# Attention into a feed-forward layer in float32: k of the first batch on ScalarE's queue, units laid out by segment first, the last stores cut into 32 rows

## The chip, the cores and the metric

The kernel runs on one core of one Trainium2 chip. The metric is device time in microseconds, the median of several executions. One execution was also taken by the hardware profiler. Its page and its trace are what is read here. The engines are called as in the profile: PE (matrix engine), PEld (its weight loads), DVE, ACT, POOL, and SP, which only issues transfers. "SPq" and "ACTq" are the queues of these engines' sequencers.

## What is computed

The inputs are q, k and v of 8 batches, 8 heads, 576 tokens and 64 channels. Two attentions are added and go through a feed-forward layer:

```python
q_d = q.reshape(B, H, Sd, factor, D).mean(axis=3)      # factor 4, the same for k and v
out_d = sm_attn(q_d, k_d, v_d)                         # attention of the means of 4 tokens
out_up = np.repeat(out_d, factor, axis=2)
mask = np.abs(pos[:, None] - pos[None, :]) < factor    # a window of 7 keys
scores = np.where(mask, scale * np.matmul(q, k.transpose(0, 1, 3, 2)), -1000000000.0)
...
x = (out_up + out_local).transpose(0, 2, 1, 3).reshape(B * S, H * D)
h = x @ w_in                                           # 512 -> 2048
g = np.maximum(h, 0.0) + alpha * np.minimum(h, 0.0)
out = g @ w_out                                        # 2048 -> 512
```

w_in and w_out come as 64-bit floats and are turned into pairs of 32-bit halves (high and low) on the chip.

## The kernel before, in words

**Layer.** The 4608 tokens are taken in 18 chunks of 256 (T), and the 2048 hidden channels in 8 pairs of 128, so 144 steps. A step makes h for two hidden blocks (`hidden`, L752: 24 matmuls, since the operands are split in high and low parts: xh, xl, wih, wil). Then ACT (`slopes`, L760 and L761), DVE (`larger`, L764) and ACT and POOL (`split`, L769 and the helper at L69) make gh and gl. `product` (L796) adds 12 matmuls into the chunk's two banks o (m = 0 and m = 1, 128 tokens each). After the eighth step of a chunk, `finish` copies both banks to sg on ACT (L802) and stores them on SP (L805). `rows` turns a stretch of tokens into addresses of the output. From token 576 on, tokens stand in units of 192, six runs of 32, so a store of 128 tokens has an address of three dimensions: 4 runs, 32 rows, 512 channels.

**Local attention.** Batch 0 is done at the start by PE (`first_batch`, four pairs of heads hp). The other batches are done by DVE in 21 units (u = 3 to 23) of 192 tokens. A unit has 128 partitions: four pairs of heads times 32 segments of 18 tokens. `load_q` and `load_kv` (L533, L552) load it, one transfer for each head of a pair (h2). `local` multiplies (L591), sums (L595) and weighs; PE transposes the result (`flip`, tile xp), and `join` (L671) adds the down part and writes xf, from which ACT and POOL make xh and xl. The first and last tokens of a sequence are masked by `build_masks`, which finds the partitions of the first and last segment.

**Down part.** `down` loads q, k and v of two heads in six transfers (tile ld, L232). POOL adds the groups of four tokens (`fold`, L72), and PE, ACT and DVE do the attention of the means.

**Start.** `load_pair` loads q, k (tile fqk, L393, runs of 64 channels) and v (fv, L396) of a pair of heads, `load_windows` the windows of v (vw). `ORDER` gives the order among these loads and those of the raw weights (L145, L149). ACT starts the decoding of the weights (temp, L184), and DVE does most of the rest (L188 to L211).

**What sets the order.** Up to the call of `tc.manual_schedule` a list scheduler places the instructions on each engine by its own estimate of times. Behind it, `events` is a list of times written out by hand, and every engine's order follows it. All transfers are issued by SP, in one order.

Of the kernel before, what the change touches and what calls it, by code (L numbers as in the profile page):

```python
# [50 lines left out]
def tile_attention_moe(ctx: ExitStack, tc: tile.TileContext, q, k, v, w_in, w_out, alpha, out):  # L51
# [29 lines left out]
    masks = {}  # L81

    def build_masks():
        for side, base in (("l", 0), ("r", -31)):
            pat = one.tile([128, 2, 7, 2, 3], F32, tag="lex", name=f"pat_{side}")
            nc.gpsimd.memset(pat, 0.0)
            for half in range(2):
                for dl in range(7):
                    js = [j for j in range(3)
                          if (3 * half + j + dl < 3 if side == "l" else 3 * half + j + dl >= 9)]  # L90
                    if js:
                        nc.gpsimd.memset(pat[:, half, dl, :, js[0]:js[-1] + 1], NEG)
            flag = one.tile([128, 4], F32, tag="flag", name=f"flag_{side}")
            nc.gpsimd.memset(flag, 0.0)
            nc.gpsimd.affine_select(out=flag, in_=flag, pattern=[[-32, 4]], base=base,
                                    channel_multiplier=1, compare_op=ALU.not_equal, fill=1.0)
            fl = one.tile([128, 1], F32, tag="fl", name=f"fl_{side}")
            nc.vector.tensor_reduce(out=fl, in_=flag, axis=AX.X, op=ALU.max)
            m = const.tile([128, 2, 7, 6], F32, name=f"mask_{side}")
            nc.vector.tensor_scalar(m.rearrange("p a b c -> p (a b c)"),  # L100
                                    pat.rearrange("p a b c d -> p (a b c d)"),
                                    fl[:, 0:1], None, op0=ALU.mult)
            masks[side] = m
# [259 lines left out]
    def first_batch(st):  # L363
# [25 lines left out]
        def load_pair(hp):  # L389
            qk[hp] = one.tile([72, 2, 8, 2, 64], F32, tag=f"spare{(4, 5, 0, 1)[hp]}", name=f"fqk{hp}")  # L390
            for i, src in enumerate((q, k)):
                for e in range(2):
                    nc.sync.dma_start(qk[hp][:, i, :, e, :],  # L393
                                      bass.AP(src.tensor, (2 * hp + e) * HEAD, [[512, 72], [64, 8], [1, 64]]))
            vt[hp] = st.tile([72, 2, 8, 64], F32, tag="vt", name=f"fv{hp}", bufs=3)
            nc.sync.dma_start(vt[hp].rearrange("p h t d -> p h (t d)"),  # L396
                              bass.AP(v.tensor, 2 * hp * HEAD, [[512, 72], [HEAD, 2], [1, 512]]))
# [132 lines left out]
    def load_q(u):  # L530
        qt = tiles[u, "q"] = late.tile([128, 2, 6, 64], F32, tag="qt", name=f"q{u}")
        for h2 in range(2):
            nc.sync.dma_start(qt[:, h2].rearrange("p t d -> p (t d)"),  # L533
                              bass.AP(q.tensor, unit_base(u) + h2 * HEAD,
                                      [[2 * HEAD, 4], [SEG * D, 32], [1, 384]]))

    def load_kv(u, x):
        src = k if x == "k" else v
        t = tiles[u, x] = late.tile([128, 2, 12, 64], F32, tag=f"{x}t", name=f"{x}{u}")
        for h2 in range(2):  # L540
            off = unit_base(u) + h2 * HEAD - 3 * D
            flat = t[:, h2].rearrange("p t d -> p (t d)")
            if u == 3 * B - 1 and h2 == 1:
                nc.vector.memset(flat[96:128, 576:768], 0.0)
                nc.sync.dma_start(flat[0:96], bass.AP(src.tensor, off,
                                                      [[2 * HEAD, 3], [SEG * D, 32], [1, 768]]))
                nc.sync.dma_start(flat[96:127], bass.AP(src.tensor, off + 6 * HEAD,
                                                        [[SEG * D, 31], [1, 768]]))
                nc.sync.dma_start(flat[127:128, 0:576],
                                  bass.AP(src.tensor, off + 6 * HEAD + 31 * SEG * D, [[1, 1], [1, 576]]))  # L550
            else:
                nc.sync.dma_start(flat, bass.AP(src.tensor, off,  # L552
                                                [[2 * HEAD, 4], [SEG * D, 32], [1, 768]]))

    def window(t, half, d0, nd):
        tok = 3 * half + d0
# [9 lines left out]
    def local(u, t0, t1):  # L566
# [94 lines left out]
        def join(i):  # L661
            j0, nt = groups[i]
            odv = od[b].rearrange("p a (s g) -> p a s g", g=9)
            tp = st.pop(("tp", i))
            xf = late.tile([128, 512], F32, tag="xf", name=f"xf{u}_{i}")[:, :128 * nt]
            xf = st["xf", i] = xf.rearrange("p (a t s) -> p a t s", a=4, s=32)
            for par in range(2):
                pos = [(18 * par + 6 * jj + j) // 4 for j in range(j0, j0 + nt)]
                for g in sorted(set(pos)):
                    k0, nk = pos.index(g), pos.count(g)  # L670
                    nc.vector.tensor_tensor(  # L671
                        xf.rearrange("p a t (s e) -> p e t a s", e=2)[:, par, k0:k0 + nk],
                        tp.rearrange("p (t a s e) -> p e t a s", t=4, a=4, e=2)[:, par, k0:k0 + nk],
                        odv[:, :, :, g].unsqueeze(1).to_broadcast([128, nk, 4, 16]), op=ALU.add)

        def place(i, low):
# [109 lines left out]
    def product(st):  # L786
        c, fp = divmod(st, NP)
        if fp == 0:
            outs[c] = [ps_o.tile([128, DM], F32, tag="po", name=f"o{c}_{m}") for m in range(T // 128)]
        gh, gl = gs.pop(st)  # L790
        for j in range(2):
            f = 2 * fp + j
            n, o = divmod(f, 4)
            for i, (g, w) in enumerate(((gh, 0), (gh, 1), (gl, 0))):
                for m, po in enumerate(outs[c]):
                    nc.tensor.matmul(po, g[:, j, 128 * m:128 * m + 128], wo[w][n][:, o, :],  # L796
                                     start=(f == 0 and i == 0), stop=(f == NF - 1 and i == 2))

    def finish(c):
        for m, po in enumerate(outs.pop(c)):  # L800
            sg = two.tile([128, DM], F32, tag="stage", name=f"sg{c}_{m}", bufs=SB)
            nc.scalar.copy(sg, po)  # L802
            row = 0
            for cnt, ap in rows(T * c + 128 * m, 128):
                nc.sync.dma_start(ap, sg[row:row + cnt, :])  # L805
                row += cnt

    def place_rest():
        hi, lo = (t[:, :, 0:S - 2 * T] for t in operand(2))
# [9 lines left out]
    with tc.tile_pool(name="start", bufs=1) as start:  # L819
# [20 lines left out]
        def at(t, f, *args):  # L840
            events.append((t, len(events), f, args))
# [5 lines left out]
    for s in range(NS):  # L847
        at(s - 1.95, hidden, s)
        at(s - 1.45, slopes, s)
        at(s - 1.15, larger, s)  # L850
        at(s - 1.0, split, s)
        at(s + 0.6, product, s)
        if s % NP == NP - 1:
            at(s + 1.02, finish, s // NP)

    blocks = [(w, fp, c) for w in range(2) for fp in range(N_EARLY, NP) for c in range(2)]
    at(-1.98, load_raw, 0, N_EARLY)
# [71 lines left out]
```

## Time and profile before

| | |
|---|---|
| median of three runs | 1025.86 us (1025.6 to 1030.05) |
| the profiled execution | 1026.39 us |
| its span, first to last instruction | 1024.5 us |
| PE busy | 960.5 us (94%) |
| DVE busy | 831.8 us (81%) |
| ACT busy | 560.4 us (55%) |
| POOL busy | 487.7 us (48%) |
| hardware queue of the transfers | 97.12 MB, 30.1% of 16 engines' span |
| granted clock of PE, mean | 0.969 |

The span is shorter than the execution's own time by what lies before the first and behind the last instruction, 1.9 us. A busy share is a mean over stages with different limits: the first 100 us (loads, decoding, batch 0), the long middle, and the last steps, in which only the layer is left. In a row of the trace stand the start, the duration, the engine, the line, the operation with its tiles and shapes, how many instructions are merged, and in brackets the idle time before it with what ended it. "A <- B" among the waits means that A's instruction stood until B's was done. A row of a stretch gives its length, the busy time of PE, PEld, DVE, ACT and POOL with their instructions, the granted clock, the mean busy share of the 16 DMA engines, and GB/s.

### The profile page before, as it was taken

To read this page: it belongs to the slowest core of one execution; us is meant where nothing else is said; L and a number is where in the kernel's file an instruction comes from. 1 tells how busy PE (TensorE), PEld (TensorE's weight loads), DVE (VectorE), ACT (ScalarE), POOL (GpSimd) and SP (SyncE) were. 2 spreads that over 40 slices of the span, in tenths; PEclk is the share of its full clock that TensorE was granted. 3 is DMA by queue.
4 is the path that set the end of the run, shared out by engine and by line. 5 is a ranking of instruction groups with operands and counts; after the bars stand their busy time and mean duration, and the time that the engine had idled before them with its cause. 6 is when DMAs were issued, how large, how long until landed. Compare 5 with 4: busy or idle time off the path is not lost.

```text
span 1024.5 us, 17852 instructions
## 1 busy us (share of the span) xinstructions
PE 960.5 (94%) x6402; PEld 853.0 (83%) x6402; DVE 831.8 (81%) x1346; ACT 560.4 (55%) x1484; POOL 487.7 (48%) x612
## 2 busy tenths in 40 slices
PE   4877989999999999999999999999999999999995
PEld 4756868898888899988888888888888898989894
DVE  6899978898788899899879888898898899995110
ACT  4767766465555554555555554655555564444442
POOL 2160645676565645555555544655555542333221
PEclk9956989999999999999999999999999999999998
DMA  8947343232322322322322232322322221100000
GB/s 184 228 141 246 111 126 110 96 109 85 115 100 95 106 75 86 109 93 102 107 84 74 92 107 77 116 90 80 104 98 81 93 78 62 73 36 21 1 21 20
DMA packets 59549, 98.25 MB, mean 96 GB/s; under 512 B 19910, under 2 KB 25286, under 8 KB 59462
## 3 DMA queue, kind: packets, MB, share of 16 engines
q1 hardware_dynamic: 59462, 97.12, 30.1%
q8 instruction: 50, 0.82, 0.3%
q14 instruction: 37, 0.30, 0.1%
HBM read 87.67 MB, written 9.44 MB: 95 GB/s over the span
## 4 chain that ended last, share of the span: by engine, by line
PE 74%; DVE 12%; DMA 4%; ACT 3%; issue 2%; SPq 2%; POOL 2%; ACTq 0%; DVEq 0%; POOLq 0%
PE h L752 34%; PE o L796 33%; PE s L263 2%; PE pv L297 2%; DVE temp L193 2%; DMA raw<-in_moe_w_in 1%; PE xp L659 1%; DMA ld<-in_v 1%; PE pT L287 1%; DVE temp L194 1%; DMA k<-in_k 1%; DVE t L764 1%; DVE qk L591 1%; SPq L393 1%; DVE temp L188 1%
## 5 line engine op out<-in xcount | busy, mean ns | idle before, releaser
L69 POOL TENSOR_TENSOR gl<-t,gh 128x512 fp32r<-128x512 f32 x144 | 186.4, 1295 | 312.9 <-ACT gh L769 281.5
L760 ACT ACTIVATE t<-h,slope 128x256 f32<-128x256 f32 x288 | 136.3, 473 | 205.4 <-PE h L752 163.6
L72 POOL TENSOR_TENSOR ld<-ld 72x256 f32<-72x256 f32 x168 | 130.8, 779 | 158.4 <-DMA ld<-in_q 88.6
L752 PE MATMUL h<-xh,wih 128*128 128x256 f32 x1152 | 191.9, 288 | 0.7 <-ACT xh L518 0.7
L764 DVE TENSOR_TENSOR t<-h,t 128x512 f32<-128x512 f32 x144 | 99.0, 687 | 114.8 <-ACT h L761 112.9
L796 PE MATMUL o<-woh,gh 128*128 128x512 f32 x576 | 187.5, 407 | 0.4 <-ACT woh L203 0.4
L752 PE MATMUL h<-xl,wih 128*128 128x256 f32 x1152 | 184.3, 282 | 1.4 <-POOL xl L69 1.4
L752 PE MATMUL h<-xh,wil 128*128 128x256 f32 x1152 | 185.0, 283 | 0.0
L796 PE MATMUL o<-woh,gl 128*128 128x512 f32 x576 | 181.1, 396 | 0.9 <-POOL gl L69 0.9
L796 PE MATMUL o<-wol,gh 128*128 128x512 f32 x576 | 181.4, 396 | 0.2 <-DVE wol L211 0.2
L752 PEld LDWEIGHTS h<-xh,wih 128*128 128x128 f32 x1152 | 164.2, 191 | 10.7 <-issue 1.8
L752 PEld LDWEIGHTS h<-xl,wih 128*128 128x128 f32 x1152 | 157.5, 190 | 1.6 <-POOL xl L69 1.6
L752 PEld LDWEIGHTS h<-xh,wil 128*128 128x128 f32 x1152 | 158.4, 191 | 0.0
L769 ACT CAST gh<-t 128x512 fp32r<-128x512 f32 x144 | 89.1, 619 | 120.7 <-DVE t L764 71.4
L595 DVE TENSOR_REDUCE ls<-qk 128x12 f32<-128x768 f32 (+1 forms) x126 | 136.4, 1082 | 2.8
L796 PEld LDWEIGHTS o<-woh,gl 128*128 128x128 f32 x576 | 108.2, 188 | 27.5 <-POOL gl L69 1.3
L796 PEld LDWEIGHTS o<-wol,gh 128*128 128x128 f32 x576 | 108.1, 188 | 26.8 <-DVE wol L211 1.1
L761 ACT ACTIVATE h<-h,sign 128x256 f32<-128x256 f32 x288 | 126.4, 439 | 0.0
L650 DVE TENSOR_TENSOR lb<-lb,pv 128x384 f32<-128x384 f32 x202 | 113.9, 564 | 5.5
L796 PEld LDWEIGHTS o<-woh,gh 128*128 128x128 f32 x576 | 98.1, 189 | 16.2 <-issue 2.2
L647 DVE TENSOR_TENSOR pv<-v,lb 128x1152 f32<-128x1152 f32 x84 | 93.6, 1115 | 2.6
L591 DVE TENSOR_TENSOR qk<-k,qp 128x768 f32<-128x768 f32 (+1 forms) x78 | 84.1, 1079 | 0.6 <-DMA k<-in_k 0.6
(146 smaller groups left out, 1108.6 us busy)
## 6 DMA issues: line engine op xcount, KB each, us to landing
k<-in_k SPq DMA_DIRECT2D x41, 384.0 KB
v<-in_v SPq DMA_DIRECT2D x41, 384.0 KB
raw<-in_moe_w_in SPq DMA_DIRECT2D x16, 512.0 KB
raw<-in_moe_w_out SPq DMA_DIRECT2D x16, 512.0 KB
ld<-in_q SPq DMA_DIRECT2D x56, 144.0 KB
ld<-in_k SPq DMA_DIRECT2D x56, 144.0 KB
ld<-in_v SPq DMA_DIRECT2D x56, 144.0 KB
q<-in_q SPq DMA_DIRECT2D x42, 192.0 KB
```

What stands on the lines that cost most here:

```text
L69: nc.gpsimd.tensor_tensor(o, a, b, op=ALU.subtract)
L72: nc.gpsimd.tensor_tensor(o, a, b, op=ALU.add)
L591: nc.vector.tensor_tensor(st["pr"][:, :nd], window(tiles[u, "k"], half, d0, nd), st["qp", half].unsqueeze(1).to_broadcast([128, nd, 2, 192 ...
L595: nc.vector.tensor_reduce(out=st["s"][:, half, d0:d0 + nd, :].rearrange("p a b -> p (a b)"), in_=st["pr"][:, :nd].rearrange("p a h (t d) - ...
L647: nc.vector.tensor_tensor(st["pr"][:, :nd], window4(tiles[u, "v"], half, d0, nd), prob(half, d0, nd), op=ALU.mult)
L650: nc.vector.tensor_tensor(st["acc"], st["acc"], st["pr"][:, i], op=ALU.add)
L752: nc.tensor.matmul(ph[:, j], w[:, m, 128 * o:128 * o + 128], x[:, m, :], start=(i == 0), stop=(i == 11))
L760: nc.scalar.activation(t[:, j], hs[st][:, j], AF.Copy, scale=slope[:, f:f + 1])
L761: nc.scalar.activation(hs[st][:, j], hs[st][:, j], AF.Copy, scale=sign[:, f:f + 1])
L764: nc.vector.tensor_tensor(gs[st], hs.pop(st), gs[st], op=ALU.max)
L769: nc.scalar.copy(gh, t)
L796: nc.tensor.matmul(po, g[:, j, 128 * m:128 * m + 128], wo[w][n][:, o, :], start=(f == 0 and i == 0), stop=(f == NF - 1 and i == 2))
```

## The change

Three edits go together.

1. In `load_pair` the two transfers of k for each pair of heads are issued by ACT instead of SP; q and v stay on SP.
2. A unit's 128 partitions are numbered by segment first and pair of heads second (partition = 4 x segment + pair, before 32 x pair + segment). The addresses of `load_q` and `load_kv` have 32 as their outer count instead of 4. The masks mark partitions 0 to 3 and 124 to 127, `join` reads the transposed tile with the matching steps, and the last unit's odd load is cut in another place.
3. In the last step `product` does all matmuls of m = 0 before those of m = 1. `finish_last` stores the last chunk: m = 0 is copied by ACT, m = 1 by DVE, and each is stored in four transfers of 32 rows, by turns on SP and ACT.

```diff
-        for side, base in (("l", 0), ("r", -31)):
+        for side, base in (("l", 0), ("r", -124)):
...
-            nc.gpsimd.affine_select(out=flag, in_=flag, pattern=[[-32, 4]], base=base,
+            nc.gpsimd.affine_select(out=flag, in_=flag, pattern=[[-1, 4]], base=base,
...
             for i, src in enumerate((q, k)):
                 for e in range(2):
-                    nc.sync.dma_start(qk[hp][:, i, :, e, :],
-                                      bass.AP(src.tensor, (2 * hp + e) * HEAD, [[512, 72], [64, 8], [1, 64]]))
+                    queue = (nc.sync, nc.scalar)[i]
+                    queue.dma_start(qk[hp][:, i, :, e, :],
+                                    bass.AP(src.tensor, (2 * hp + e) * HEAD, [[512, 72], [64, 8], [1, 64]]))
...
             nc.sync.dma_start(qt[:, h2].rearrange("p t d -> p (t d)"),
                               bass.AP(q.tensor, unit_base(u) + h2 * HEAD,
-                                      [[2 * HEAD, 4], [SEG * D, 32], [1, 384]]))
+                                      [[SEG * D, 32], [2 * HEAD, 4], [1, 384]]))
...
-                nc.sync.dma_start(flat[0:96], bass.AP(src.tensor, off,
-                                                      [[2 * HEAD, 3], [SEG * D, 32], [1, 768]]))
-                nc.sync.dma_start(flat[96:127], bass.AP(src.tensor, off + 6 * HEAD,
-                                                        [[SEG * D, 31], [1, 768]]))
+                for s0, n in ((0, 16), (16, 15)):
+                    nc.sync.dma_start(flat[4 * s0:4 * (s0 + n)],
+                                      bass.AP(src.tensor, off + s0 * SEG * D, [[SEG * D, n], [2 * HEAD, 4], [1, 768]]))
+                nc.sync.dma_start(flat[124:127], bass.AP(src.tensor, off + 31 * SEG * D, [[2 * HEAD, 3], [1, 768]]))
...
                 nc.sync.dma_start(flat, bass.AP(src.tensor, off,
-                                                [[2 * HEAD, 4], [SEG * D, 32], [1, 768]]))
+                                                [[SEG * D, 32], [2 * HEAD, 4], [1, 768]]))
...
-                        tp.rearrange("p (t a s e) -> p e t a s", t=4, a=4, e=2)[:, par, k0:k0 + nk],
+                        tp.rearrange("p (t s e a) -> p e t a s", t=4, a=4, e=2)[:, par, k0:k0 + nk],
...
+        order = [(j, i, m) for j in range(2) for i in range(3) for m in range(T // 128)]
+        if st == NS - 1:
+            order.sort(key=lambda x: x[2])
+        for j, i, m in order:
...
+    def finish_last(c):
+        for m, po in enumerate(outs.pop(c)):
+            sg = two.tile([128, DM], F32, tag="stage", name=f"sg{c}_{m}", bufs=SB)
+            if m == 0:
+                nc.scalar.copy(sg, po)
+            else:
+                nc.vector.tensor_copy(sg, po)
+            for i in range(4):
+                (_, ap), = rows(T * c + 128 * m + 32 * i, 32)
+                (nc.sync if i % 2 == 0 else nc.scalar).dma_start(ap, sg[32 * i:32 * i + 32, :])
...
-            at(s + 1.02, finish, s // NP)
+            at(s + 1.02, finish if s + 1 < NS else finish_last, s // NP)
```

The hand-written order of the middle is the same before and after. The start is placed anew by the list scheduler, on every engine. Three places show it. First, ACT's first instructions in the program before (raw_0_122 is the first block of w_in, f0T the transposed q of a pair):

```order
L378 ACT_TABLE_LOAD
L378 CAST unit<-ident 128x128
L184 ACTIVATE temp<-raw_0_122 128x1024
L376 CAST wmask<-wpat 128x630
L429 COPY qb<-f0T_179 64x9x8x4 x2
```

and ACT's first instructions in the changed one (fqk_125, 132, 147 and 157 are the four pairs of heads):

```order
L394 DMA fqk_125<-in_k 72x8x64 x2
L378 ACT_TABLE_LOAD
L378 CAST unit<-ident 128x128
L394 DMA fqk_132<-in_k 72x8x64 x2
L394 DMA fqk_147<-in_k 72x8x64
L376 CAST wmask<-wpat 128x630
L394 DMA fqk_147<-in_k 72x8x64
L394 DMA fqk_157<-in_k 72x8x64 x2
L184 ACTIVATE temp<-raw_0_122 128x1024
```

All eight issues of k, of all four pairs, now stand ahead of the first temp, and five of them ahead of wmask.

Second, DVE in the start, where it takes the fourth pair's v (fv_162) and the first block of w_out (raw_0_144), before:

```order
L193 SCALAR_TENSOR_TENSOR temp<-raw_0_144,temp 128x1024
L471 TENSOR_TENSOR fv_152<-fv_152 72x4x128
L194 SCALAR_TENSOR_TENSOR temp<-raw_0_144,temp 128x1024
L481 TENSOR_REDUCE fmx_421<-fs_380 128x7
L481 TENSOR_REDUCE fmx_421<-fs_389 128x2
L482 TENSOR_TENSOR fp_424<-fs_380,fmx_421 128x490
L211 SCALAR_TENSOR_TENSOR wol_83<-temp,sign,woh_82 128x512
L482 TENSOR_TENSOR fp_424<-fs_389,fmx_421 128x140
L211 SCALAR_TENSOR_TENSOR wol_83<-temp,sign,woh_82 128x512
L471 TENSOR_TENSOR fv_162<-fv_162 72x4x128
```

and DVE at the same place in the changed program (its lines are one further on):

```order
L193 SCALAR_TENSOR_TENSOR temp<-raw_0_144,temp 128x1024
L482 TENSOR_REDUCE fmx_421<-fs_380 128x7
L482 TENSOR_REDUCE fmx_421<-fs_389 128x2
L194 SCALAR_TENSOR_TENSOR temp<-raw_0_144,temp 128x1024
L472 TENSOR_TENSOR fv_162<-fv_162 72x4x128
L483 TENSOR_TENSOR fp_424<-fs_380,fmx_421 128x490
L483 TENSOR_TENSOR fp_424<-fs_389,fmx_421 128x140
L211 SCALAR_TENSOR_TENSOR wol_83<-temp,sign,woh_82 128x512
```

fv_162 has moved ahead of the two subtractions into fp_424 and of both L211.

Third, the end of ACT's program (sg_0 and sg_1 are the copies of the last chunk's two banks), before:

```order
L760 ACTIVATE t_11877<-h_11852,slope 128x256
L761 ACTIVATE h_11852<-h_11852,sign 128x256
L769 CAST gh_11895<-t_11877 128x512
L802 COPY sg_0_11923<-o_0_11645 128x512
L802 COPY sg_1_11927<-o_1_11646 128x512
```

and the end of ACT's program in the changed one:

```order
L761 ACTIVATE t_11879<-h_11854,slope 128x256
L762 ACTIVATE h_11854<-h_11854,sign 128x256
L770 CAST gh_11897<-t_11879 128x512
L816 COPY sg_0_11925<-o_0_11647 128x512
L821 DMA out<-sg_0_11925 32x512 x2
L821 DMA out<-sg_1_11931 32x512 x2
```

ACT's second copy has gone to DVE, as its last instruction, and ACT issues two stores of each half; SP issues the other two of each in place of three larger ones.

More of the change, by code (lines that the diff above doesn't have):

```diff
@@ L790, in product @@
         gh, gl = gs.pop(st)
-        for j in range(2):
+        order = [(j, i, m) for j in range(2) for i in range(3) for m in range(T // 128)]
+        if st == NS - 1:
+            order.sort(key=lambda x: x[2])
+        for j, i, m in order:
             f = 2 * fp + j
             n, o = divmod(f, 4)
[L794 to L797, printed above, removed]
+            g, w = ((gh, 0), (gh, 1), (gl, 0))[i]
+            nc.tensor.matmul(outs[c][m], g[:, j, 128 * m:128 * m + 128], wo[w][n][:, o, :],
+                             start=(f == 0 and i == 0), stop=(f == NF - 1 and i == 2))
     def finish(c):
```

## The prediction

> **What bounds the kernel now.** I read the page first, then the rows by stage, then the end, then the waits. The page's chain of work that ended last, with its shares of the span by engine, and its stages (busy us and instructions of PE, PEld, DVE, ACT and POOL, then the granted clock, the DMA share and GB/s):
>
> ```profile
> PE 74%; DVE 12%; DMA 4%; ACT 3%; issue 2%; SPq 2%; POOL 2%; ACTq 0%; DVEq 0%; POOLq 0%
> ...
> 0.00:10.00 10.00, 0.21 (x2) 0.24 (x3) 4.83 (x15) 3.31 (x4) 5.60 (x26) 1.00 0.76 163
> 10.00:40.00 30.00, 24.94 (x169) 22.12 (x169) 23.16 (x42) 17.70 (x46) 0.00 (x0) 1.00 0.99 199
> ...
> 50.00:100.00 50.00, 35.46 (x240) 29.63 (x241) 49.65 (x76) 32.92 (x78) 19.08 (x12) 0.59 0.54 184
> ...
> 165.00:264.00 99.00, 94.32 (x641) 84.16 (x639) 89.71 (x152) 54.51 (x155) 68.07 (x88) 1.00 0.29 98
> ...
> 165.00:1012.40 847.40, 833.02 (x5548) 744.20 (x5546) 690.25 (x1112) 450.17 (x1212) 428.40 (x527) 1.00 0.25 82
> ```
>
> There are three regimes. Up to 40 us the DMA engines are full (a share of 0.99 from 10 us on), and DVE idles 40 - (4.83 + 23.16) = 12.0 us. From 50 to 100 us DVE is the bound: 49.65 of 50. From 165 to 1012.4 us PE is: 833.0 of 847.4 us, so only 14.4 us of PE idle are to be had there. The end is a fourth thing: PE has finished at 1012.4, and 12.1 us follow.
>
> **The change part by part: the end.** Last matmuls (start, duration), copies, store issues, then the stretches behind them, and a DVE row that reads PSUM:
>
> ```profile
> 1011.32 0.63 PE L796 MATMUL o<-wol,gh 128*128 128x512 f32 x2
> 1011.78 0.62 PE L796 MATMUL o<-woh,gl 128*128 128x512 f32 x2
> 1012.22 1.07 ACT L802 COPY sg<-o 128x512 f32<-128x512 f32 x2 [4.95 <-PE o L796]
> 1012.83 1.79 SPq L805 DMA_DIRECT2D out<-sg  x3
> ...
> 1012.50:1014.00 1.50, 0.00 (x0) 0.00 (x0) 0.00 (x0) 0.79 (x2) 0.00 (x0) 1.00 0.00 0
> 1014.00:1015.50 1.50, 0.00 (x0) 0.00 (x0) 0.00 (x0) 0.00 (x0) 0.00 (x0) 0.70 0.11 18
> ...
> 1015.50:1023.20 7.70, 0.00 (x0) 0.00 (x0) 0.00 (x0) 0.00 (x0) 0.00 (x0) 0.50 0.20 65
> ...
> 1023.20:1024.50 1.30, 0.00 (x0) 0.00 (x0) 0.00 (x0) 0.00 (x0) 0.00 (x0) 0.50 0.00 0
> ...
> L764 DVE TENSOR_TENSOR t<-h,t 128x512 f32<-128x512 f32 x144 | 99.0, 687 | 114.8 <-ACT h L761 112.9
> ```
>
> The three stores move 512 KB from 1014.0 to 1023.2, in 9.2 us, at 65 GB/s once they run, on a share of 0.20: about three engines of 16. Their addresses have 2 or 4 as the outer count. A transfer of 32 rows has 32 there, so I expect all 16. New end: a pair of matmuls takes 1011.78 - 1011.32 = 0.46 us, so m = 0, now first, is done 6 x 0.23 = 1.4 us before the other, at 1011.0. ACT copies it by 1011.6 (1.07 / 2 = 0.54 us), and its two issues on SP and two on ACT (1.79 / 3 = 0.6 us each) end by 1012.8, hidden behind PE and the second copy. m = 1 is done at 1012.4. DVE's copy from PSUM has no row; it lies between ACT's 0.54 and t's 0.69 us, which reads two operands, I take 0.65, so 1013.1. Two issues per queue: the last starts at 1013.7. From issue to first packet it is 1014.0 - 1012.8 = 1.2 us, so 1014.9. The data then: 0.2 us at the weights' rate (row below) up to the 1.5 us in which the old stores ran at 18 GB/s; I take 1.1, so 1016.0. Behind the last packet stay 1.3 us: 1017.3. **Gain 7.2 us.** With everything at its best (copy 0.54, data 0.2, issues of 0.55) 8.2; with ACT's issues at 1.4 us each (mean below), the last ACT issue starts at 1011.6 + 3 x 1.4 = 1015.8 and the end is 1019.4, gain 5.1.
>
> [...]
>
> **The unit loads.** A lone k load of a late unit, a stretch of it; a weight load for comparison; then the sums of waits on loads (us, times, longest), waits behind POOL, and PE's own stalls:
>
> ```profile
> 852.39 1.13 SPq L552 DMA_DIRECT2D k<-in_k  x2
> ...
> 861.00:862.00 1.00, 1.00 (x9) 0.95 (x8) 0.93 (x3) 0.37 (x2) 1.00 (x1) 1.00 0.25 98
> ...
> 64.00:65.00 1.00, 0.81 (x5) 0.39 (x3) 1.00 (x2) 1.00 (x3) 1.00 (x2) 0.50 0.88 324
> ...
> POOL ld L72 <- DMA ld<-in_v: 62.4, 16, 12.6
> POOL ld L72 <- DMA ld<-in_q: 46.7, 15, 6.9
> POOL ld L72 <- DMA ld<-in_k: 7.3, 6, 3.3
> ...
> DVE xf L671 <- POOL xl L69: 5.4, 3, 2.6
> DVE x L653 <- POOL pv L72: 2.2, 2, 1.7
> DVE qk L591 <- DMA k<-in_k: 0.6, 2, 0.3
> DVE lb L643 <- DMA v<-in_v: 0.6, 1, 0.6
> ...
> 254.04 0.74 PE L752 MATMUL h<-xl,wih 128*128 128x256 f32 x4 [1.43 <-POOL xl L69]
> 264.32 0.41 PE L287 MATMUL pT<-ident,dp 96*72 96x96 f32 x3 [1.85 <-DVE xf L671]
> ```
>
> The 768 KB come on a share of 0.25, four engines, at 98 GB/s: about 8 us. With 32 as the outer count all engines can serve, and at the weights' 324 GB/s it is 2.4 us. DVE itself waits for k and v only 0.6 + 0.6 us. What counts more is queued behind them: the ld loads of the down part, for which POOL stood 116.4 us, with gl and xl behind it in order. Most of that costs nothing, since PE is the bound; of the waits behind POOL, DVE's come to 5.4 + 2.2 us, PE's to 1.43 and part of 1.85. I take **3 us of gain**, nearest to these two stalls; the bounds are 0 (all hidden) and 10 (the DVE rows with k and v, 8.8, and PE's 1.43). Once loads stop being late there, the next to be late is DVE (89.71 of 99 us from 165 on).
>
> The join reads the same PSUM tile with a step of 8 elements instead of 2:
>
> ```profile
> L671 DVE TENSOR_TENSOR xf<-xp,od 128x128 f32<-128x128 f32 x74 | 26.0, 387 | 6.2 <-POOL xl L69 5.4 <-ACT qp L585 0.7 <-PE xp L659 0.2
> ...
> L671 DVE TENSOR_TENSOR xf<-xp,od 128x256 f32<-128x256 f32 x16 | 10.1, 630 | 0.4 <-PE xp L659 0.4
> ```
>
> It pays (630 - 387) / 128 = 1.9 ns an element already, more than t's 687 ns for 512, so the strided rate is being paid; I take no difference. Half as much again would be 18 us of DVE spread over 21 units, mostly in its idle time.
>
> **The start.** SP's eight k issues (min/median/max ns) and in pairs, the ACT rows that now stand behind them, and DVE's waits up to 40 us:
>
> ```profile
> L393 SPq DMA_DIRECT2D fqk<-in_k x8: 792/942/2826, 4.8 to 30.1; - x8
> ...
> 4.76 2.86 SPq L393 DMA_DIRECT2D fqk<-in_k  x2
> 10.26 2.69 SPq L393 DMA_DIRECT2D fqk<-in_k  x2
> 20.46 3.66 SPq L393 DMA_DIRECT2D fqk<-in_k  x2
> 29.08 1.93 SPq L393 DMA_DIRECT2D fqk<-in_k  x2
> ...
> 0.73 1.28 ACT L378 ACT_TABLE_LOAD   x1 [0.73 <-PEq L916]
> 2.14 0.30 ACT L378 CAST unit<-ident 128x128 fp32r<-128x128 f32 x1
> 7.80 1.12 ACT L184 ACTIVATE temp<-raw 128x1024 f32<-128x1024 f32 x1 [5.36 <-DMA raw<-in_moe_w_in]
> 8.81 0.71 ACT L376 CAST wmask<-wpat 128x630 fp32r<-128x630 f32 x1
> ...
> DVE fv L471 <- DMA fv<-in_v: 5.4, 3, 2.6
> DVE temp L188 <- ACT temp L184: 3.0, 2, 2.0
> ```
>
> SP is rid of eight issues, 2.86 + 2.69 + 3.66 + 1.93 = 11.1 us. That opens little: the DMA engines have only 2.4 us free in the first ten and 0.3 in the next thirty, so the **best case is a gain of 3 us**. The bytes are the same, and all of k now goes ahead of w_out and of the later q and v. On ACT eight issues stand ahead of the first temp (L184). At 0.8 to 1.4 us each (median to mean) they take 6.4 to 11.2, and with the table, two casts (1.0 us) and the start at 0.73, temp begins at 9.4 to 14.2 instead of 7.80: 1.6 to 6.4 us late, and DVE's first L188 with it. Behind it DVE waited about 6 us more for fv and the second temp; if those data land as before, that slack swallows the delay. On DVE the last fv, for which it waited 2.6 us, now stands ahead of two L483 and two L211, about 2.4 us of work that used to come before that wait. I take **a loss of 1.5 us**, between 3 gained and 6 lost; DVE is full from 40 to 100 us, so what is lost there stays.
>
> [...]
>
> **Sum.** -7.2 - 3.0 + 1.5 = -8.7 us. The profiled execution took 1026.39 us (span 1024.5), so 1017.7; it lies 0.5 above the median of 1025.86, so **1017.2 us**.
>
> **The rivals.**
> - Loads were worth more: all 10 us, and no loss at the start: 1025.9 - 17.2 = 1008.7. For it: 116.4 us of POOL standing. Against: PE's 14.4 us of idle have other causes too.
> - The start takes it back: 6 lost, loads 0: 1025.9 - 7.2 + 6 = 1024.7. For it: DVE full from 40 us on.
> - It doesn't spread: 32 rows and the new loads still use four engines. The stores then run from 1012.8 for 512 KB / 64 GB/s = 8.2 us, the end is 1022.3, gain 2.2; with the start 1025.2.
> - Slower: an issue on ACT costs p = 2.83 us, the longest of the eight k issues, because its queue is held up. At the start temp is 8p + 3.0 - 7.8 late, less 6.1 of slack: 8p - 10.9. At the end ACT's fourth issue starts at 1011.6 + 3p, so the gain is 9.3 - 3p. With 3 for the loads the sum is 11p - 23.2: it turns at p = 2.1 and passes 0.5% at 2.6; at 2.83 it is +7.9, so 1033.8 us. Against: half of the eight took 0.94 us or less on SP.
>
> **How the numbers follow.** Forecast 0.66, more from loads 0.12, start takes it back 0.12, no spread 0.05, slower 0.05. About 0.5% (5.1 us) is what a measurement of this kernel tells from no change. Under 1020.8 lie the first two less 0.01: faster 0.77; same 0.18; slower 0.05. The forecast's bounds and the nearer parts of the rivals give 1011 to 1023.
>
> **What would show it.** End: the store share well above 0.25 and the span ending about 5 us behind the last matmul. Loads: a lone k load in about 3 us, POOL's waits on ld under half of 116, PE's stalls at 254 and 264 gone. Start: first L184 at 9 to 14 us, DVE full from about 38. I am wrong if ACT's issues exceed 2 us, if the new transfers stay at a share of 0.25, or if xf rows grow.

## The result and the profile after

| kernel | runs | median us | lowest to highest | ratio to before, 95% |
|---|---|---|---|---|
| before | 5 | 1030.05 | 1025.6 to 1035.75 | |
| changed | 5 | 1019.63 | 1015.02 to 1021.57 | 0.9898 (0.9867 to 0.9929) |

The change makes the kernel about 1% faster. The profiled execution of the changed kernel took 1018.09 us with a span of 1016.3 us (before: 1026.39 and 1024.5). The runs of either kernel spread by 0.6 to 1%, so the two profiles, one execution each, can't be set against each other to the microsecond; where the spread comes from is part of what the experiments showed.

The page's chain of the changed kernel, and the stages that were shown of before (busy us and instructions of PE, PEld, DVE, ACT and POOL, granted clock, DMA share, GB/s):

```profile
PE 74%; DVE 14%; ACT 4%; issue 2%; DMA 2%; POOL 2%; ACTq 1%; SPq 0%; DVEq 0%; POOLq 0%
```

```profile
0.00:10.00 10.00, 0.75 (x2) 0.50 (x2) 3.42 (x13) 2.30 (x3) 5.70 (x26) 1.00 0.74 170
10.00:40.00 30.00, 23.79 (x165) 21.43 (x165) 23.88 (x43) 18.39 (x45) 0.00 (x0) 1.00 1.02 215
50.00:100.00 50.00, 42.50 (x305) 34.10 (x304) 49.62 (x79) 37.29 (x90) 14.84 (x11) 0.67 0.54 188
165.00:1012.10 847.10, 834.45 (x5549) 745.58 (x5547) 691.03 (x1112) 451.62 (x1213) 429.01 (x527) 1.00 0.27 83
```

(The clock of 1.00 up to 40 us is taken up again in the last section.) The three regimes are the same: DMA full to 40 us, DVE full from 50 to 100, PE the bound from 165 on. PE still idles 847.1 - 834.5 = 12.6 us there (14.4 before).

The end, from the timeline of the changed kernel (start, duration) and by stretches behind the last matmul:

```profile
1010.79 0.59 ACT L816 COPY sg<-o 128x512 f32<-128x512 f32 x1 [3.78 <-PE o L799]
1011.40 2.30 SPq L821 DMA_DIRECT2D out<-sg  x4
1011.40 2.36 ACTq L821 DMA_DIRECT2D out<-sg  x4
1011.75 0.40 PE L799 MATMUL o<-woh,gl 128*128 128x512 f32 x1
1012.19 0.69 DVE L818 COPY sg<-o 128x512 f32<-128x512 f32 x1 [5.89 <-PE o L799]
```

```profile
1012.30:1013.50 1.20, 0.00 (x0) 0.00 (x0) 0.58 (x1) 0.00 (x0) 0.00 (x0) 1.00 0.81 205
1013.50:1015.00 1.50, 0.00 (x0) 0.00 (x0) 0.00 (x0) 0.00 (x0) 0.00 (x0) 1.00 0.69 175
1015.00:1016.30 1.30, 0.00 (x0) 0.00 (x0) 0.00 (x0) 0.00 (x0) 0.00 (x0) 0.58 0.00 0
```

The last matmul ends at 1011.75 + 0.40 = 1012.15, and 4.15 us follow (12.1 before). The stores run on a share of 0.7 to 0.8 at 175 to 205 GB/s, where the old ones had 0.20 and 65 GB/s.

A lone k load of a late unit, issued at 852.40 (before: a share of 0.25 from 855 to 862):

```profile
853.00:854.00 1.00, 1.00 (x11) 1.00 (x11) 0.97 (x2) 0.62 (x1) 0.23 (x1) 1.00 0.42 52
854.00:855.00 1.00, 1.00 (x11) 1.00 (x10) 1.00 (x1) 0.00 (x0) 1.00 (x1) 1.00 0.74 233
855.00:856.00 1.00, 1.00 (x10) 0.96 (x9) 0.93 (x5) 0.24 (x1) 0.06 (x1) 1.00 1.04 413
856.00:857.00 1.00, 1.00 (x6) 0.82 (x5) 0.93 (x6) 0.60 (x3) 0.00 (x0) 1.00 0.26 89
```

The 768 KB are in by 857, in 3 to 4 us instead of 9. POOL's waits on ld from 100 us on fell from 116.4 to 33.8 us (sum, times, longest), and the join's rows did not grow (387 and 630 ns before):

```profile
POOL ld L72 <- DMA ld<-in_v: 20.2, 5, 6.3
POOL ld L72 <- DMA ld<-in_q: 10.2, 4, 4.0
POOL ld L72 <- DMA ld<-in_k: 3.4, 1, 3.4
...
L672 DVE TENSOR_TENSOR xf<-xp,od 128x128 f32<-128x128 f32 x74 | 25.9, 387 | 6.2 <-POOL xl L69 5.4 <-ACT qp L586 0.7
L672 DVE TENSOR_TENSOR xf<-xp,od 128x256 f32<-128x256 f32 x16 | 10.1, 632 | 0.4 <-PE xp L660 0.4
```

PE's own stalls of the changed kernel near the places that were shown of before (1.43 us at 254, 1.85 at 264), and a longer one that both kernels have near 533 us:

```profile
253.38 0.74 PE L753 MATMUL h<-xl,wih 128*128 128x256 f32 x4 [0.59 <-POOL xl L69]
263.67 0.44 PE L287 MATMUL pT<-ident,dp 96*72 96x96 f32 x3 [1.88 <-ACT th L291]
533.22 0.41 PE L287 MATMUL pT<-ident,dp 96*72 96x96 f32 x3 [2.44 <-DVE lb L617]
```

Two further stalls of before, of which the first has no counterpart in the changed kernel:

```profile
601.72 0.74 PE L796 MATMUL o<-woh,gl 128*128 128x512 f32 x2 [0.87 <-POOL gl L69]
...
532.34 0.41 PE L287 MATMUL pT<-ident,dp 96*72 96x96 f32 x3 [2.50 <-DVE lb L616]
```

So the first stall shrank, the second kept its size and changed its releaser (DVE's xf before, ACT's th now), and one near 602 us that the prediction had not counted went.

The start, ACT's timeline in the changed kernel:

```profile
0.74 2.26 ACTq L394 DMA_DIRECT2D fqk<-in_k  x2
...
5.40 3.04 ACTq L394 DMA_DIRECT2D fqk<-in_k  x1
8.48 0.72 ACT L376 CAST wmask<-wpat 128x630 fp32r<-128x630 f32 x1 [3.86 <-issue]
9.74 3.97 ACTq L394 DMA_DIRECT2D fqk<-in_k  x3
13.83 1.12 ACT L184 ACTIVATE temp<-raw 128x1024 f32<-128x1024 f32 x1 [4.63 <-DMA fv<-in_v]
```

The eight issues (two more of them, 2.27 us, lie between the first two rows) took 2.26 + 2.27 + 3.04 + 3.97 = 11.5 us, 1.4 each, and the first temp came at 13.83 instead of 7.80. Yet the first step of the hidden layer on DVE (t, the row below) began at 89.8 us instead of 92.9, and the sixth at the same time as before.

### The profile page after: what moved, and what is told of

Its sections match the earlier page's. It is cut to its first block, busy times and chain, and to the rows that moved or that the text cites. A ratio compares the mean times of both kernels' runs of the same rounds, so it can differ in the third digit from the quotient of the medians.

```text
span 1016.3 us, 17860 instructions
## 1 busy us (share of the span) xinstructions
PE 965.5 (95%) x6402; PEld 856.0 (84%) x6402; DVE 832.0 (82%) x1347; ACT 561.7 (55%) x1483; POOL 487.5 (48%) x612
## 4 chain that ended last, share of the span: by engine, by line
PE 74%; DVE 14%; ACT 4%; issue 2%; DMA 2%; POOL 2%; ACTq 1%; SPq 0%; DVEq 0%; POOLq 0%
PE h L753 34%; PE o L799 33%; PE s L263 2%; PE pv L297 2%; DVE lb L651 1%; DVE t L765 1%; DMA ld<-in_q 1%; DVE qk L592 1%; DVE ls L596 1%; DVE pv L648 1%; PE xp L660 1%; PE pT L287 1%; DVE temp L193 1%; DVE temp L194 1%; ACT t L761 1%
## 5 line engine op out<-in xcount | busy, mean ns | idle before, releaser
L72 POOL TENSOR_TENSOR ld<-ld 72x256 f32<-72x256 f32 x168 | 126.2, 752 | 73.0 <-DMA ld<-in_q 49.3
L648 DVE TENSOR_TENSOR pv<-v,lb 128x1152 f32<-128x1152 f32 x84 | 93.6, 1114 | 2.6
```

Of the source, the lines that this page charges most:

```text
L72: nc.gpsimd.tensor_tensor(o, a, b, op=ALU.add)
L648: nc.vector.tensor_tensor(st["pr"][:, :nd], window4(tiles[u, "v"], half, d0, nd), prob(half, d0, nd), op=ALU.mult)
```

## The experiments

Times are medians, set against the kernel before as measured beside them on the same chip; its medians there were 1028.95, 1027.42 and 1027.89 us.

### The three parts alone, and two of them together

Four kernels split the change. `e_tail` has only the third edit (the end), `e_loads` only the second (masks, load_q, load_kv, join), `e_kact` only the first:

```diff
-                    nc.sync.dma_start(qk[hp][:, i, :, e, :],
+                    queue = (nc.sync, nc.scalar)[i]
+                    queue.dma_start(qk[hp][:, i, :, e, :],
```

`e_no_kact` is the changed kernel without these lines, k back on SP's queue.

> The kernel before with the last chunk's end alone (m = 0 first, DVE's copy, stores of 32 rows in turn on SP and ACT). Theory A (the end is all of the gain, the two profiles' middle and start cancel): the span ends about 4.2 us behind the last matmul instead of 12.1, the time is 7.9 us under before, ratio 0.992, and this kernel stands level with the changed one. Theory B (the loads and the start bring some 2 to 4 us in the mean that the one pair of profiles hides): also -7.9 here, but 2 to 4 us above the changed kernel (ratio of the changed kernel was 0.990). Theory C (the start's lead is absorbed by 106 us): no difference from A here.

> The kernel before with the units' partitions by segment first alone (masks, load_q, load_kv, join). POOL's waits on ld loads fall from 116 to about 34 us, as in the changed kernel, and a lone k load goes from 8 to about 3 us. Theory A: time within 1 us of before (ratio 0.999 to 1.001). Theory B: 2 to 4 us faster (0.996 to 0.998), with PE idling less between 165 and 1012 us. The prediction's 3.0 us would be 0.997.

> The kernel before with the first batch's k on ScalarE's queue alone. The first temp (L184) comes near 13.8 us instead of 7.8, and DVE's first t (h, L764) about 3 us earlier (89.8 instead of 92.9). Theory A and C: that lead is gone by 106 us, time within 1 us of before. Theory B: 1 to 3 us faster. The prediction's step: 1.5 us slower (1.0015).

> The changed kernel with k of the first batch back on SyncE's queue (end and unit loads remain). Theory A and C: level with the changed kernel and with the end alone, ratio 0.992 to before. Theory B: what the start brings is missing, 1 to 3 us above the changed kernel. The prediction's step (start costs 1.5): 1.5 us under the changed kernel, 0.9885 to before.

| kernel | runs | median us | ratio to before, 95% |
|---|---|---|---|
| e_tail | 12 | 1020.93 | 0.9930 (0.9907 to 0.9954) |
| e_loads | 12 | 1022.07 | 0.9956 (0.9936 to 0.9976) |
| e_kact | 12 | 1030.95 | 1.0017 (0.9993 to 1.0041) |
| e_no_kact | 5 | 1014.56 | 0.9866 (0.9843 to 0.9888) |

In us of 1029: the end -7.2, the loads -4.5, k on ACT +1.7 (its interval takes in 0). The three add to -10.0, which is what the changed kernel gained in its first five runs (1030.05 - 1019.63 = 10.4). Theory A falls: the loads bring more than half as much as the end, though the two first profiles hid it. Theory B holds for the loads and falls for the start, which doesn't gain. Theory C, that a lead of some 3 us at the first t is gone by 106 us, had nothing to work on in e_kact: its first t came at 91.8 us, against 92.9 before. The kernel with k left on SP is the fastest of the five.

### Why one pair of profiles hid the loads: stalls that lower the clock

DVE's t (one per step of the hidden layer) cuts a span into pieces. Its rows between 147 us and the end, first and last start at the end of the numbers; first before, then e_tail, e_no_kact and the changed kernel:

```profile
L764 DVE TENSOR_TENSOR t<-h,t x136: 675/691/715, 151.6 to 1005.9; 128x512 f32<-128x512 f32 x136
```

```profile
L764 DVE TENSOR_TENSOR t<-h,t x136: 676/692/693, 149.5 to 1010.0; 128x512 f32<-128x512 f32 x136
```

```profile
L764 DVE TENSOR_TENSOR t<-h,t x136: 675/692/694, 151.8 to 1002.1; 128x512 f32<-128x512 f32 x136
```

```profile
L765 DVE TENSOR_TENSOR t<-h,t x136: 676/691/694, 151.8 to 1005.6; 128x512 f32<-128x512 f32 x136
```

The same 136 steps took 854.3, 860.5, 850.3 and 853.8 us. In e_loads they took 850.2, and 850.2 to 850.6 in every later kernel that had the loads by segment and no phase of the kind that follows; this is what PE needs with the stalls that all of them keep. What is above it lies in longer stalls, and behind some of them. The longest one of e_tail, from its timeline:

```profile
602.74 0.73 PE L798 MATMUL o<-woh,gl 128*128 128x512 f32 x2 [2.55 <-POOL gl L69]
```

The 3.4 us behind the stall at 263.67 of the changed kernel, and behind this one of e_tail, by stretches:

```profile
264.40:267.60 3.20, 3.20 (x9) 2.43 (x9) 3.13 (x4) 0.56 (x2) 0.00 (x0) 0.50 0.01 2
```

```profile
603.40:606.80 3.40, 3.40 (x12) 2.71 (x11) 2.28 (x3) 1.96 (x5) 2.37 (x3) 0.50 0.26 99
```

The granted clock is 0.50 for about 3.4 us, and PE does about half the work in it (9 matmuls in 3.20 us, against 20 in the 3.20 us of after_again at 1.00 below): an estimated 3.4 x 0.5 = 1.7 us lost beside the stall itself. Read by stage, e_tail has four such phases in its middle (near 262, 532, 603 and 689 us), the changed kernel two, before one, e_loads and e_no_kact none. With 1.7 us for each phase and the extra length of the stalls that the timelines list, what the 136 steps took above 850.2 us comes out to within 0.5 us in every profile (in e_tail 10.3 us: 6.8 for the phases and 3.8 for stalls).

A stall isn't always followed by a phase: the same stall of 2.43 to 2.52 us near 532 us was followed by one in six of the thirteen profiles of this case and not in the others, and the changed kernel's second profile (after_again, below) had the stall of 1.88 us near 264 with the clock at 1.00 behind it:

```profile
265.50:268.70 3.20, 3.20 (x20) 2.60 (x18) 3.17 (x4) 1.35 (x4) 0.00 (x0) 1.00 0.08 29
```

What decides it can be read from the traces. In each profile the phases begin and end on a grid of 3.41 us, which lies elsewhere in each, and fill whole cells of it (in the changed kernel's clock record they start at 264.27 and 533.92 us, 79 cells apart, and last 3.41 us each). Near 532 us, two cells of the changed kernel, then three of after_again:

```profile
530.51:533.92 3.41, 0.96 (x11) 0.79 (x9) 3.20 (x11) 1.90 (x6) 2.29 (x3) 1.00 0.52 170
533.92:537.33 3.41, 3.41 (x18) 3.41 (x18) 2.09 (x3) 0.19 (x1) 2.66 (x4) 0.50 0.47 148
```

```profile
528.05:531.46 3.41, 2.79 (x14) 2.01 (x12) 1.96 (x4) 2.77 (x8) 2.79 (x4) 1.00 0.31 89
531.46:534.87 3.41, 1.58 (x15) 1.61 (x16) 3.13 (x12) 1.68 (x5) 2.81 (x4) 1.00 0.61 202
534.87:538.29 3.42, 3.42 (x24) 3.05 (x23) 1.27 (x1) 1.62 (x4) 2.28 (x4) 1.00 0.31 100
```

In the changed kernel the whole stall lies in one cell (PE idle for 3.41 - 0.96 = 2.45 us), and the next cell has the clock at 0.50. In after_again it is split into 0.62 and 1.83 us, and no phase follows; of its 1.88 us near 264, 1.78 lie in one cell. From 170 to 1005 us the thirteen profiles have 14 phases. All eleven cells at full clock with 1.84 us or more of PE idle time were followed by one, and so was one cell with 1.81 us; one cell with 1.83 and two with 1.78 us were not, nor any with less, except two with 1.41 us (e_tail and e_kact, near 688 us). So in these profiles the bound lies near 1.8 us of idle time within one cell, and whether a stall of about 2 us passes it depends on where it falls on the grid. Why the two cells with 1.41 us passed stays open.

So the loads' gain has two parts: shorter stalls behind POOL (near 254 from 1.43, 1.05 and 0.94 us in the three kernels with old loads to 0.57 to 0.61 in the nine with the loads by segment; near 602 from 0.87, 2.55 and 1.08 to none), and fewer half-clock phases. The phases near 532 us are no part of it: the stall there is the same in all kernels, and its place on the grid decides.

### Is it the outer count, or the new partition order?

`e_split32` keeps the old partition order and masks, has the new end, and cuts each unit load into four transfers of 32 rows:

```diff
-                nc.sync.dma_start(flat, bass.AP(src.tensor, off,
-                                                [[2 * HEAD, 4], [SEG * D, 32], [1, 768]]))
+                for a in range(4):
+                    nc.sync.dma_start(flat[32 * a:32 * a + 32],
+                                      bass.AP(src.tensor, off + 2 * a * HEAD, [[SEG * D, 32], [1, 768]]))
...
```

> The kernel before with the new end, its old partition order, and every unit load of q, k and v cut into four transfers of 32 rows (32 as the outer count, four times as many issues on SyncE). Theory F (the gain of the unit loads comes of the outer count alone): a k load runs on all engines, POOL's waits on ld fall from 116 to 30 to 45 us, the stall near 602 us is gone, and the time stands level with the changed kernel without k on ScalarE's queue, ratio 0.987 to 0.990, less what the longer issue on SyncE gives back (18 more issues a unit at some 0.5 us, 9 us of a queue that has one unit in some 35 us). Theory G (the partition order itself does it, by the join or the masks): waits stay near 116 us and the ratio is that of the new end alone, 0.993.

It took 1016.69 us, ratio 0.9883 (0.9849 to 0.9918), and its waits on ld from 100 us on are

```profile
POOL ld L72 <- DMA ld<-in_v: 24.3, 5, 6.8
POOL ld L72 <- DMA ld<-in_q: 11.3, 6, 3.4
...
POOL ld L72 <- DMA ld<-in_k: 3.6, 1, 3.6
```

39.2 us together, and the stall near 602 is gone. Theory F holds for the waits and, within the interval, for the time: 32 as the outer count is enough. Whether the partition order adds something isn't settled: PE's stalls near 254 and 264 us stayed longer here (0.77 and 1.84 us) than with the loads by segment and the same bank (0.57 to 0.61 and 1.47 to 1.49). In the lone k load of a late unit, an outer count of 4 went with a share of 0.25 (before) and one of 32 with a share up to 1.04 (changed). What the extra issues of e_split32 cost SP doesn't show in the time within its interval; its profile had three half-clock phases in the middle, and the 136 steps took 855.6 us.

### What k on ScalarE's queue costs, and where

The changed kernel and e_no_kact ran once more side by side, with a third kernel. Between the first two, from about 130 us on, every engine has the same instructions in the same order; one of the few differences left is which PSUM bank the transpose pT near 264 us is given. With k on SP it gets the one that DVE's xf frees, with k on ACT the one that ACT's th frees. `e_bank` is the changed kernel with the two th copies placed slightly later in the table. On PE, DVE and POOL no order changes by it; on ACT the cast of xh now runs ahead of the two copies, which the expectation below didn't foresee. pT gets the first bank:

```diff
-            at(t1 + pace * lag, f, *args)
+            late_th = 0.15 if (b, hp) == (2, 2) and f is turned else 0
+            at(t1 + pace * lag + late_th, f, *args)
```

> The changed kernel once more, beside its variants on one chip. If k on ScalarE's queue costs what the first four runs say, its ratio to before is again near 0.990, 3.3 us above the kernel with k back on SyncE's queue. If that difference came of the chip alone, the two stand level here.

> The changed kernel with k of the first batch on SyncE's queue, once more. Theory D (k on ScalarE's queue costs something): ratio 0.9866 again, 3.3 us under the changed kernel. Theory E (chance of chip or run): level with it.

> The changed kernel with one thing more: the two th copies of the down part of batch 2, pair 2 are placed 0.15 of a step later in the table, which leaves every engine's order as it is and gives the transpose pT (L287) near 264 us the PSUM bank that DVE's xf frees (as it has with k on SyncE's queue) instead of the one that ACT's th copy frees. Theory D1 (half or more of what k on ScalarE's queue costs is this bank): the stall near 264 us goes from 1.88 to 1.47 us, the 3.4 us at half clock behind it go, worth 0.4 + 1.7 = 2.1 us: ratio 0.988. Theory D2 (the cost lies in the start): the stall shrinks, the time stays, 0.990.

| kernel | runs | median us | lowest to highest | ratio to before, 95% |
|---|---|---|---|---|
| after_again | 6 | 1020.93 | 1016.55 to 1024.07 | 0.9931 (0.9908 to 0.9955) |
| e_bank | 6 | 1017.88 | 1017.52 to 1018.32 | 0.9904 (0.9885 to 0.9923) |
| e_no_kact_again | 6 | 1016.15 | 1013.71 to 1019.35 | 0.9890 (0.9865 to 0.9914) |

The difference came back: 0.0041, or 4.2 us (3.3 in the first comparison). e_bank takes 2.8 of them, and in its profile the stall is

```profile
267.02 0.41 PE L287 MATMUL pT<-ident,dp 96*72 96x96 f32 x3 [1.48 <-DVE xf L673]
```

instead of 1.88, with the clock at 1.00 behind it. The place of the cast isn't what shortens it: e_no_kact has 1.47 us with ACT's order as in the changed kernel. So a change of the first 15 us made a stall at 264 us longer, by the choice of a buffer. What that is worth is less sure. e_bank's ratio is the 0.990 that was expected under D2, and only against the changed kernel's 0.9931 here does it gain 2.8 us; the intervals overlap, and in the profile of after_again, which has no phase, the 136 steps took just 0.4 us longer than in e_bank's. D1 is likely rather than settled; the shorter stall is read directly.

The rest, as far as the traces show it, stands in the start. Rows of t between 85 and 130 us, in e_no_kact, in the changed kernel, and in e_kact:

```profile
L764 DVE TENSOR_TENSOR t<-h,t x6: 681/684/684, 92.1 to 125.3; 128x512 f32<-128x512 f32 x6
```

```profile
L765 DVE TENSOR_TENSOR t<-h,t x6: 681/684/692, 89.8 to 125.5; 128x512 f32<-128x512 f32 x6
```

```profile
L765 DVE TENSOR_TENSOR t<-h,t x6: 677/684/692, 91.8 to 128.3; 128x512 f32<-128x512 f32 x6
```

From the first t to the sixth it is 33.2, 35.7 and 36.5 us. This hardly varies: 32.7 to 33.2 in all nine profiles with k on SP, 35.7 to 36.5 in all four with k on ACT. The first t comes 0.7 us earlier in the mean with k on ACT (92.0 against 92.7), which is little beside the spread (89.8 to 93.6 against 90.0 to 95.5); the 89.8 of the first pair, on which the expectation of e_kact rested, didn't come back. The sixth comes 2.2 us later in the mean (127.9 against 125.7). The sure part is the 2.5 to 3.8 us lost between the two. There ACT's order differs: a decode of a weight block (L184) that stands ahead of the first step's activations with k on SP has moved in between them:

```
-L184 ACTIVATE temp<-raw_4_869 128x1024
 L519 CAST xh_327<-fxs_783 128x256
 L761 ACTIVATE t_995<-h_970,slope 128x256
 L762 ACTIVATE h_970<-h_970,sign 128x256
+L184 ACTIVATE temp<-raw_4_869 128x1024
 L761 ACTIVATE t_995<-h_970,slope 128x256
```

(Minus: k on SP, plus: k on ACT.) It is one of several differences in the orders of ACT and DVE up to about 105 us. That this one causes the 3 us is argued from where it stands; no run put it back alone.

### The end, taken apart

Three kernels vary the end of e_no_kact, whose span ends 4.1 us behind its last matmul. `t_32` keeps the spread stores but not the early m = 0 nor DVE's copy; `t_early` keeps these two but not the stores; `t_sp` keeps all and issues all eight stores on SP. Their edits, in this order:

```diff
-        if st == NS - 1:
-            order.sort(key=lambda x: x[2])
...
-            if m == 0:
-                nc.scalar.copy(sg, po)
-            else:
-                nc.vector.tensor_copy(sg, po)
+            nc.scalar.copy(sg, po)
```

```diff
-            for i in range(4):
-                (_, ap), = rows(T * c + 128 * m + 32 * i, 32)
-                (nc.sync if i % 2 == 0 else nc.scalar).dma_start(ap, sg[32 * i:32 * i + 32, :])
+            row = 0
+            for cnt, ap in rows(T * c + 128 * m, 128):
+                nc.sync.dma_start(ap, sg[row:row + cnt, :])
+                row += cnt
```

```diff
-                (nc.sync if i % 2 == 0 else nc.scalar).dma_start(ap, sg[32 * i:32 * i + 32, :])
+                nc.sync.dma_start(ap, sg[32 * i:32 * i + 32, :])
```

> The changed kernel with k on SyncE's queue, and of its end only the stores of 32 rows on two queues: m = 0 and m = 1 finish together again and ACT copies both. If the stores' spread carries the end's gain: the span ends 5.1 us behind the last matmul (about 1 more than 4.15, ACT's second copy standing behind two issues). If the early m = 0 and DVE's copy carry it: 9 us or more.

> The changed kernel with k on SyncE's queue, and of its end m = 0 first and DVE's copy, with the old stores of whole halves on SyncE's queue. If the stores' spread carries the end's gain: the 512 KB again take 8 to 9 us at 65 GB/s, from about 1.0 us behind the last matmul on (SyncE's first issue is 1.4 us earlier), and the span ends 10.5 to 11.2 us behind the last matmul instead of 12.1. If the early m = 0 carries it: 5 to 6 us.

> The changed kernel with k on SyncE's queue, and all eight last stores on SyncE's queue too. Eight issues of 0.37 us from 0.75 us ahead of the last matmul's end; the last then starts 1.85 us behind it instead of 1.15: the span ends 4.85 us behind the last matmul, 0.7 more than with two queues. If issue time hides wholly: 4.15. [...]

| | last matmul ends | span ends | behind it |
|---|---|---|---|
| before | 1012.4 | 1024.5 | 12.1 |
| t_early | 1006.16 | 1016.8 | 10.6 |
| t_32 | 1008.16 | 1013.8 | 5.6 |
| t_sp | 1009.92 | 1015.1 | 5.2 |
| e_no_kact | 1008.63 | 1012.7 | 4.1 |

The stores' spread alone is worth 12.1 - 5.6 = 6.5 us, the early m = 0 with DVE's copy 12.1 - 10.6 = 1.5, and both 8.0. The second queue is worth 1.1 us (0.7 expected) by one profile of each. That is a rough figure: e_tail's profile, with the whole new end, ended 4.9 us behind its last matmul (4.2 expected), the six others with that end 4.0 to 4.1. SP's eight issues in a row:

```profile
1009.16 3.64 SPq L820 DMA_DIRECT2D out<-sg  x8
```

In t_early the old stores run as before, at a share of 0.20, over 7.5 us:

```profile
1008.00:1015.50 7.50, 0.00 (x0) 0.00 (x0) 0.00 (x0) 0.00 (x0) 0.00 (x0) 0.58 0.20 66
```

Each of these three ran once, so their times stand beside the others only roughly (1015.72, 1018.64 and 1016.83 us); the stretch behind the last matmul is read within one profile.

## Why the prediction was right, and where not

**The total.** -8.7 us was forecast; the two comparisons gave ratios of 0.9898 and 0.9931, -10.5 and -7.1 us of 1029. The time of 1019.63 lies in the range, 2.4 above the 1017.2. That the total came so near is in part luck: the loads gained 1.5 us more than was put down for them, and k on ACT cost 1.8 to 2.7 us more.

**The end (-7.2).** Right in mechanism and size: e_tail alone has -7.2 us, and the stretch behind the last matmul shrank by 7.9. Its best case of 8.2 adds up to 8.3. Two terms of it were off, in opposite directions. An issue took 0.41 us on ACT (row below), not 0.6, so the first half's data were moving by 1012.3, right behind the last matmul. Then they ran for 2.7 us, until 1015.0, at 175 to 205 GB/s, rather than for 1.1 us behind the last issue. The tile's row for ACT's issues in the changed kernel (shortest, median and longest in ns, first and last start):

```profile
L821 ACTq DMA_DIRECT2D out<-sg x4: 375/414/435, 1011.4 to 1013.3; - x4
```

In t_sp the eight transfers of 64 KB on one queue took 1015.1 - 1009.16 = 5.9 us from the first issue to the end of the span, the wait for the second half included.

**The unit loads (-3.0).** The mechanism held: on a share up to 1.04 instead of 0.25, the lone k load takes 3 to 4 us, POOL's waits fall to 29% and PE's stalls behind POOL shrink. The size was too small: -4.5 us, still within the bounds. The step that failed is the price of a stall. The prediction took 1.43 us and part of 1.85 as what they cost. The stall near 254 kept 0.6 us and the one near 264 did not go (1.88 us, or 1.47 to 1.49 with xf's bank); one near 602, 0.87 to 2.55 us long in the kernels with old loads, went instead; and the half-clock phases, about 1.7 us each, had no place in the sum.

**The start (+1.5).** The size came near (+1.7 alone, with an interval from -0.7 to +4.2), but by luck, since the place was another. The prediction put the loss on the first temp and on DVE up to 40 us. Two of its signs came true: temp at 13.83, inside 9 to 14, and DVE's last wait for fv small (2.6 us before, 0.17 now). A third didn't: DVE was to be full from about 38 us, and was busy for 8.53 of the 10 us from 40 on (10.00 before). All this was swallowed by the first t, which came no later (92.0 against 92.7 us in the mean). The loss lies between 90 and 125 us, where the list scheduler laid ACT's decodes otherwise (argued, not tested), and in part at 264 us in a PSUM bank. In the changed kernel k on ACT costs 3.3 to 4.2 us, more than twice the term. "The hand-written order of the middle is the same", in the section on the change, held for the order and not for the buffers.

**The rivals.** "The start takes it back" is half true: the start does cost more in the changed kernel, but the loads do bring their part. "It doesn't spread" and "an issue on ACT costs 2.83 us" fall by the rows above: single issues at the start did take 3.04 us, yet the mean was 1.4, and 0.41 at the end.

## What to carry to other kernels

In this kernel the share of the DMA engines that a transfer got went with its outer count (lone k load, 4: 0.25, 32: up to 1.04; last stores, 2 or 4: 0.20, 32: 0.69 to 0.81): look for DMA shares of 0.20 or 0.25 in stretches with one transfer, which at the program's end are time itself, and in the middle are time only through the stall at the end of their chain. Price a stall of PE of about 2 us with the half-clock phase that can follow it (here 1.7 us more, when some 1.8 us of it fell into one cell of the grid), and don't read a gain of a few us from one pair of profiles. Undo each part of a bundled change by itself: a scheduler carries an edit in one corner into orders and buffers far away, and here the two parts without the third are the best version (0.9866 and 0.9890 of before), level with e_split32 (0.9883).

## What the runs showed that was not expected

Runs of one kernel differ for two reasons that the traces show. The first is the half-clock phases of 3.4 us behind stalls of 1.81 to 2.55 us (twice 1.41), in some executions and not in others: in the thirteen profiles the same 136 steps took from 850.2 to 860.5 us. The lowest values, 850.2 and 850.3, came up in all six profiles with spread loads and the freed bank of xf near 264 in which no stall was followed by such a phase.

The second lies in the start, and is the larger of the two between the profiles of e_no_kact. The span of e_no_kact was 1012.7 us, of e_no_kact_again 1017.5; the first of the 136 steps came at 151.8 and 155.3 us, and the steps took 850.3 and 851.6. The same ten matmuls in the two, and the stretch around them:

```profile
39.31 1.33 PE L445 MATMUL fs<-kT,qb 128*128 128x70 f32 x10
40.00:50.00 10.00, 7.78 (x87) 5.91 (x86) 9.93 (x22) 9.33 (x27) 1.79 (x1) 0.96 1.03 269
```

```profile
41.56 2.41 PE L445 MATMUL fs<-kT,qb 128*128 128x70 f32 x10
40.00:50.00 10.00, 10.00 (x69) 9.05 (x70) 6.70 (x16) 6.05 (x20) 1.40 (x2) 1.00 0.98 259
```

In the second they took nearly twice as long, and DVE was busy for 6.70 instead of 9.93 us. The row gives a clock of 1.00, but the clock record of that trace has its first entry at 49.5 us only. In the other twelve the first entry stands at 32.6 to 37.1 us, always at 1.00. So the 1.00 in rows ahead of the first entry isn't a reading, and by these matmuls (0.24 us each against 0.13) PE ran at about half speed then. The profile of before has its first entry at 35.0 us; 18 matmuls of that line took 4.11 us from 27.46 on, 0.23 us each, and ten took 1.33 us from 39.77 on, 0.13 each. The time of the first entry differs from run to run; what sets it no run here shows.

Eight stores of 64 KB on two queues moved at 175 to 205 GB/s, while three larger ones had 65. An issue of a DMA on ACT took 0.41 us at the end, for the last two with the DMA engines at a share of 0.81, and 1.4 us in the mean (up to 3.04) in the first 14 us, when their share was 0.74 or more. The share alone doesn't explain that. The transfers differ too (k in runs of 64 channels, the stores in rows of 512); no run separates the two.
